# Which weight pieces share a slot in a recurrent attention loop, and who evacuates what

## The chip, the cores and the metric

The kernel runs on one core of a Trainium2 chip. The metric is the device time of one execution in microseconds, the median of three runs: 2337.44 us before the change (2331.31 to 2341.88). The profile is one further execution, with a span of 2344.3 us.

## What is computed

Two branches over the same 2048 tokens of 1024 features are mixed by a gate. The second branch is a plain gated feed-forward. The first is attention over segments of 32 tokens with 8 memory rows that each segment hands to the next, so its 64 segments must run one after the other:

```python
for s in range(n_seg):
    xs = x[:, s * seg_len:(s + 1) * seg_len, :].copy()
    h = jnp.concatenate([mem, xs], axis=1)          # 8 + 32 rows
    q = jnp.einsum('btd,dhe->bhte', h, Wq)          # 32 heads of 128
    k = jnp.einsum('btd,dhe->bhte', h, Wk)
    v = jnp.einsum('btd,dhe->bhte', h, Wv)
    scores = jnp.einsum('bhqe,bhke->bhqk', q, k) * scale
    scores = jnp.where(mask[None, None], scores, -1000000000.0)
    p = _softmax(scores, axis=-1)
    o = jnp.einsum('bhqk,bhke->bhqe', p, v)
    o = jnp.einsum('bhte,hed->btd', o, Wo)
    mem = o[:, :M, :].copy()
    outs.append(o[:, M:, :])
...
g = _sigmoid((x * gate_w).sum(-1, keepdims=True))
return g * a + (1 - g) * b
```

## The kernel before, in words

The program is built in Python by a small recorder (class _Prog): each call of `op` notes an engine, the regions it reads and writes, and from these the waits between engines follow. Work on one engine runs in the order in which it was recorded. Two engines that touch the same PSUM bank are always put one after the other (lines 51 to 55).

**Weights.** Each of Wq, Wk, Wv, Wo is cut into 16 pieces of 512 KB: 8 for each half of the heads (half 0 and half 1). That is 64 pieces, and on-chip memory has 52 slots for them. So 40 pieces stay for the whole loop, and 24 pieces form 12 pairs: piece i of half 0 and piece i of half 1 of the same matrix share a slot. `PAIRS` (line 318) names the paired pieces. As soon as the tensor engine has used the piece in a shared slot, `spent` (after each piece) records the load of its partner on the sync engine's queue, which is served in order. A segment walks one half, then the other; the next segment begins with the half that is in the slots, so that each pair costs one load in a segment: 12 loads, 6.3 MB.

**Order of a segment.** `walk` (line 328) lists the 64 piece steps by hand: k and q of the first half alternating (16 steps), v of the first half (8), k and q of the second half (16), then o of the first half and v of the second half alternating (16), then o of the second half (8). `seq` puts paired pieces first in the first half and last in the second half. Each step is four or eight matmuls on 32-column strips of the array (`proj`).

**What is hung between the steps.** `on(m, r, n, f)` records f ahead of step n of matrix m in half r:

- ahead of the first v step: k is copied from its PSUM bank by ScalarE (ACT), q by VectorE (DVE);
- `turn`, ahead of the fifth v step and of the first o step: k and q are transposed by the tensor engine (`trans8`, line 690), both into bank TT; ACT then copies kT, DVE copies qT (`heads`);
- `scores` and `softmax`: the score matmuls, then a chain of DVE steps with one exponential on ACT, which ends in the transposed probabilities tA (memory and most rows) and tB (the other 8 rows), lines 725 to 742;
- `attend` (line 754) and `attend_tail` (line 766), which need tA, tB and v; their results oT are copied by ACT and DVE in turn;
- "fills": work of a later group of four segments (projections of 8 rows per segment, line 830, and the last o product of earlier rows, line 849) that is independent of the recurrence. `fa` and `fb` hold 8 such steps each, and `some(fa, 2)` puts two of them at that place;
- at the end, the segment's result (bank XO) is copied to a_bf in two halves, the first by ACT and the second by DVE; its 8 memory rows are turned by an identity matmul (line 1027) into hT of the next segment.

The banks are named XO, F2, TT, SS, B0, B1, B2, F1. k goes to B0, q to B1, v of the first half to XO, v of the second half to B0. Behind the loop, the feed-forward takes slices 32 to 40 of the span; the change does not touch it, except that the pieces of Wo which shared a slot are loaded once more near the end (`load_xo`).

Of the kernel before, what the change touches and what calls it, by code (L numbers as in the profile page):

```python
# [30 lines left out]
class _Prog:  # L31
# [47 lines left out]
    def op(self, eng, fn, rd=(), wr=(), lane=None, after=()):  # L79
        o = _Op(eng, fn)  # L80
        if lane is not None:
            ln = self.lanes.get(lane)
            if ln is None:
                ln = self.lanes[lane] = [self.new_sem(f"{self.name}_{lane}"), 0, None]
            if ln[2] is not None:
                o.deps.append(ln[2])
            ln[1] += 16
            o.sem, o.val, o.inc, o.need = ln[0], ln[1], 16, True
            ln[2] = o
        for r in rd:  # L90
            self._touch(o, r, False, lane is not None)
        for r in wr:
            self._touch(o, r, True, lane is not None)
        o.deps.extend(after)
        if eng == "pool" and lane is None:
            if self.pool is not None:
                o.deps.append(self.pool)
            self.pool = o
        for d in o.deps:
            d.need = True  # L100
        o.idx = len(self.ops)
        self.ops.append(o)
        return o
# [92 lines left out]
def bass_gated_mix__memory_aug_recurrent_mem_tr__geglu_ffn__prompt_kernel(  # L196
# [35 lines left out]
    with ExitStack() as es:  # L232
# [23 lines left out]
        PB = [es.enter_context(nc.psum_tensor(f"pb{i}", [128, 512], FP32)) for i in range(8)]  # L256
        PBV = [p[:, :].bitcast(BF16) for p in PB]
# [22 lines left out]
        ident = al("ident", [128, 128])  # L280
# [9 lines left out]
        kT = al("kT", [128, 4, 4, LQ])  # L290
# [3 lines left out]
        tok = al("tok", [128, 512])  # L294
        stage = al("stg", [128, 512])
        pA = al("pA", [128, 8, 32])
        pB = al("pB", [128, 288])
        a_bf = al("a_bf", [128, 256], at=pA.off)
        vAs = [al("vA0", [128, 4, 128], at=oT.off), al("vA1", [128, 4, 128], at=tok.off)]
        qT = al("qT", [128, 4, 4, 32], at=stage.off)  # L300
        tok2 = al("tok2", [128, 512], at=oT.off + 1024)
# [12 lines left out]
        fqk = al("fqk", [128, 4, 2, 128], at=odd0)  # L314
        NSLOT = NLOW + (top - cur[0]) // PIECE


        PAIRS = {"k": (0, 2), "q": (0,), "v": (0, 1, 2, 3), "o": (0, 1, 2, 3, 4)}

        def seq(m, r):  # L320
            pairs = PAIRS[m] if m in "vo" else sorted({*PAIRS["k"], *PAIRS["q"]})
# [2 lines left out]
            return p + f if r == 0 else f + p  # L324
        both = lambda r: [(m, r, i) for i in seq("k", r) for m in "kq"]
        one = lambda m, r: [(m, r, i) for i in seq(m, r)]
        walk = both(0) + one("v", 0) + both(1) + [x for y in zip(one("o", 0), one("v", 1)) for x in y] + one("o", 1)
        spot = {}
        for p, (m, r, i) in enumerate(walk):
            spot.setdefault((m, r), []).append(p)  # L330
# [16 lines left out]
        for s_ in range(NSEG):  # L347
            for p in range(64):
                k = at_step(p, s_)
# [3 lines left out]
        op = P.op  # L353
        BK = lambda b: ("P", b)
        XO, F2, TT, SS, B0, B1, B2, F1 = range(8)
# [43 lines left out]
        for g in range(4):  # L399
            q = slice(32 * g, 32 * g + 32)  # L400
# [136 lines left out]
        def load_v(s, us=(0, 1), eng="sp"):  # L537
# [7 lines left out]
           wr=[gwb.r()], lane="gw")  # L545
# [25 lines left out]
        for T in range(TB):  # L571
            do_x(T)
            load_x(T + NPX)
            if T == 0:
                op("dve", lambda e: e.tensor_copy(hT[:, :, NR:32], memT[:, :].rearrange("p (k c) -> p k c", k=KC)),
                   rd=[memT.r()], wr=[hT.r()])
                op("dve", lambda e: e.tensor_copy(hT[:, :, 0:NR], xTp[0][:, 0, 0, :, 0:NR]),
                   rd=[xTp[0].r(0, KC * SEG)], wr=[hT.r()])
# [3 lines left out]
        for fb in range(NFB):  # L582
            for j in range(NJP):
# [8 lines left out]
                if T == NT:  # L592
                    op("act", lambda e: e.activation(gal[:, :], dl[:, :], ACTF.Exp, scale=-1.0), rd=[dl.r()], wr=[gal.r()])
                    op("dve", lambda e: e.tensor_scalar(out=dl[:, :], in0=gal[:, :], scalar1=1.0, scalar2=None, op0=ALU.add),
                       rd=[gal.r()], wr=[dl.r()])
# [79 lines left out]
        def act_copy(o, i, rd, wr):  # L675
            op("act", lambda e: e.activation(o, i, ACTF.Copy), rd=rd, wr=wr)  # L676
# [4 lines left out]
        cp = {"act": act_copy, "dve": dve_copy}  # L681

        def evac(bank, t, eng="act", lo=0, hi=512):
            cp[eng](t[:, lo:hi] if len(t.h.shape) == 2 else t[:, lo // 128:hi // 128, :].rearrange("p j c -> p (j c)"),
                    PB[bank][:, lo:hi], [BK(bank)], [t.r(lo, hi)])

        def trans4(e, t=tok, head=False, x=0):
            for j in range(4):
                to = PBV[TT][:, x:x + 512].rearrange("p (g j y) -> p j g y", g=4, j=4)[:, j] if head else PBV[TT][:, x + j * 128:x + (j + 1) * 128]
                ins = e.transpose(to, t[:, j * 128:(j + 1) * 128], ident[:, :])  # L690
            return ins

        def trans8(ka, qa, head=False):
            def f(e):
                trans4(e, ka)
                return trans4(e, qa, head, 512)
            op("pe", f, rd=[ka.r(), qa.r(), ident.r()], wr=[BK(TT)])

        def heads(to, eng, x):
            i_ap = PBV[TT][:, x:x + 512].rearrange("p (j g c) -> p (j g) c", g=4, c=32)  # L700
            cp[eng](to[:, :, :, 0:32].rearrange("p j g c -> p (j g) c"), i_ap, [BK(TT)], [to.r()])

        sS = PB[SS][:, 0:320].rearrange("p (a c) -> p a c", a=8)
        nm, sm = st8[:, 0, :], st8[:, 1, :]
# [2 lines left out]
        def scores(u):  # L707

            def f(e):
                for g in range(4):  # L710
                    q = slice(32 * g, 32 * g + 32)
                    e.matmul(PB[SS][q, 0:320].rearrange("p (a c) -> p a c", a=4), lhsT=ident[:, q],
                             rhs=mS[:, :].unsqueeze(1).to_broadcast([128, 4, 80]), start=True, stop=False, skip_group_check=True)
                for j in range(4):
                    for g in range(4):
                        e.matmul(PB[SS][32 * g:32 * g + 32, j * 80:j * 80 + LQ], lhsT=qT[:, j, g, :], rhs=kT[:, j, g, :],
                                 start=False, stop=True, skip_group_check=True)
                for g in range(4):
                    ins = e.matmul(PB[SS][32 * g:32 * g + 32, 0:320].rearrange("p (a c) -> p a c", a=4)[:, :, LQ:80],  # L719
                                   lhsT=qkr[:, u, 0, 32 * g:32 * g + 32], rhs=kT[:, :, g, :],  # L720
                                   start=False, stop=True, skip_group_check=True)
                return ins
            op("pe", f, rd=[qT.r(), kT.r(), ident.r(), mS.r(), qkr.r(256 * u, 256 * u + 128)], wr=[BK(SS)])
            op("pool", lambda e: e.memset(pB[:, :].bitcast(FP32), 0.0), wr=[pB.r()])
            op("dve", lambda e: e.tensor_reduce(nm, sS, AX.X, ALU.max, negate=True), rd=[BK(SS)], wr=[st8.r(0, 8)])  # L725
            op("dve", lambda e: e.tensor_tensor(out=sS, in0=sS, in1=b8(nm, LQ), op=ALU.add), rd=[BK(SS), st8.r(0, 8)], wr=[BK(SS)])  # L726
# [53 lines left out]
        bank_of = {("k", 0): B0, ("q", 0): B1, ("k", 1): B0, ("q", 1): B1, ("v", 0): XO, ("v", 1): B0}  # L780
# [81 lines left out]
                                                      t[32 * g:32 * g + 32, 0:256]),  # L862
                   rd=[t.r(0, 256)] + [("D", "a", x) for x in range(4 * Q, 4 * Q + 4)], wr=[("D", "ar", Q, g)], lane=f"ar{g}")

        def fill_put(ap, r, how, x=0):
            cp[how](ap.rearrange("p i (x c) -> p x i c", x=16), PBV[TT][:, x:x + 512].rearrange("p (x i c) -> p x i c", x=16, i=4),
                    [BK(TT)], [r])

        def store_v(u, G, st, eng="act"):
            op(eng, lambda e: e.dma_start(v_scr[4 * G:4 * G + 4, :, u].rearrange("s i (g j) c -> g (s i) (j c)", g=4), st[:, :]), rd=[st.r()],  # L870
# [31 lines left out]
        for s in range(NSEG):  # L902
            last = s == NSEG - 1
            at = {}
            ua, ub = s % 2, 1 - s % 2
# [9 lines left out]
            def on(m, r, n, *fs):  # L915
                at.setdefault(spot["k" if m == "q" else m, r][n], []).extend(fs)
# [6 lines left out]
            def some(fs, n=99):  # L923
                return lambda: run(fs, n)
# [40 lines left out]

            def turn():
                trans8(tok, stage)
                heads(kT, "act", 0)
                heads(qT, "dve", 512)
            on("v", 0, 4, turn)  # L970
            on("k", 1, 0, lambda: evac(bank_of["v", 0], vAs[0]))
            on("k", 1, 1, lambda: scores(ua))
            on("k", 1, 1, softmax)
            on("k", 1, 5, lambda: rest_k(ub))
            if uw is not None:
                on("k", 1, 5, lambda: load_oR(Q, uw))

            on("o", 0, 0, lambda: evac(bank_of["k", 1], tok))
            on("o", 0, 0, lambda: evac(bank_of["q", 1], stage, "dve"))
            on("o", 0, 0, some(fa, 2))  # L980
            on("o", 0, 0, lambda: attend(ua, 0))
            on("o", 0, 0, lambda: attend_tail(ua, 0))
            on("o", 0, 0, some(fa, 1))
            on("o", 0, 0, turn)
            on("o", 0, 3, lambda: scores(ub))
            on("o", 0, 3, softmax)

            def halves(bank, t):
                evac(bank, t, "act", 0, 256)
                evac(bank, t, "dve", 256, 512)  # L990
            on("o", 1, 0, lambda: halves(bank_of["v", 1], vAs[1]))
            on("o", 1, 0, some(fa))
            on("o", 1, 0, lambda: attend(ub, 1))
            on("o", 1, 0, lambda: attend_tail(ub, 1))
# [20 lines left out]
            for p in range(64):  # L1015
                run(at.get(p, []))
                proj(p, s)
            for t, eng in enumerate(("act", "dve")):
                cs = slice(128 * t, 128 * t + 128)
                cp[eng](a_bf[:, cs], PB[XO][:, cs], [BK(XO)], [a_bf.r(cs.start, cs.stop)])  # L1020
            run(fb, 2)
            if not last:
                for t, bk, eng in ((0, B2, "dve"), (1, SS, "act")):
# [17 lines left out]
            if k1:  # L1041
                pend.append((0, [lambda: evac(F1, tok2), lambda: evac(F2, tok, "dve")]))

                def fills_in(u=k1[1], G=G):
                    trans8(tok2, tok, True)
                    fill_put(fqk[:, :, 1, :], fqk.r(), "act")
                    fill_put(fqk[:, :, 0, :], fqk.r(), "dve", 512)
                    store_qk(u, G, fqk)
                pend.append((3, [fills_in]))
            if uw == 0:  # L1050
# [51 lines left out]
        for fb in range(NFB):  # L1102
            HB, DN = ((0, 1, 2, 3), (4, 5, 6, 7)) if fb % 2 == 0 else ((4, 5, 6, 7), (0, 1, 2, 3))
            for j in range(NJR):
                if fb == 0 and j == sum(CH[:2]):
                    last_tail()
                c, cc = jch[j][0], jch[j][1] * 128
# [90 lines left out]
```

## Time and profile before

| what | value | where |
|---|---|---|
| span of the profiled execution | 2344.3 us | page, head |
| mean granted tensor-engine clock | 0.960 | cores |
| loads of Wo / Wv / Wk / Wq into slots | 331 / 268 / 142 / 79, of 512 KB | page, part 6 |
| median time from issue to landing | 6.9 / 8.0 / 6.8 / 6.7 us | page, part 6 |
| matmul of 512 columns on a strip (L800) | 394 ns mean | page, part 5 |
| ACT copy of 128x512 from PSUM (L676, tok) | 598 ns | page, part 5 |
| DVE copy of 128x512 from PSUM (L679, stg) | 673 ns | page, part 5 |
| ACT and DVE copies of half a v (vA, 128x256) | 384 and 385 ns | groups by form |
| DVE copy of qT, 128x512 bf16 | 425 ns | groups by form |
| DVE idle for qT until ACT had copied kT | 131.4 us, 128 times | waits |
| DVE idle for a_bf until ACT had copied its half | 336.5 us, 64 times | waits |

The page's second part cuts the span into 40 equal slices and gives each engine's busy share in tenths; PEclk is the clock that was granted to the tensor engine, DMA the mean busy share of the 16 DMA engines. The waits view sums the idle time of an engine just ahead of a line by what ended it: total in us, how many times, and the longest. A stage table gives busy us and instruction counts of each engine in stretches of time. A busy tensor engine is not an engine at its peak: a matmul of 512 columns is shown with about 380 ns, while the next four start every 215 ns.

### The profile page before, as it was taken

What the parts mean: (1) busy time and instruction counts of PE and PEld (TensorE: products, weight loads), DVE (VectorE), ACT (ScalarE), POOL (GpSimd) and SP (SyncE); (2) the same over time, 40 slices, a digit from 0 to 9 for tenths busy, and PEclk for the clock granted to TensorE, in tenths of its full rate; (3) what the DMA queues carried; (4) which work ended last, traced back from release to release, by engine and by line L of the source; (5) the groups of instructions that cost most, each with busy time, mean ns of one, the idle gap of its engine ahead of it and who ended that gap; (6) DMA issues with size and microseconds to landing.
All of it is one profiled execution on the core that took longest, in us unless ns stands there. A gap on an engine that the chain in (4) does not pass through costs nothing.

```text
span 2344.3 us, 77525 instructions
## 1 busy us (share of the span) xinstructions
PE 2057.8 (88%) x38218; PEld 944.3 (40%) x32556; DVE 1014.3 (43%) x2248; ACT 601.1 (26%) x1266; POOL 294.1 (13%) x589
## 2 busy tenths in 40 slices
PE   7778888888888888888888888888887999999999
PEld 4334444344444444444444434344333434334343
DVE  6334443444444443444444433444334535345262
ACT  4222222222222222222222222222222312213130
POOL 7110111111111111111101111011101000000000
PEclk9989999999999999999999999999988999999999
DMA  9977787787878878787888877788779900001000
GB/s 369 353 253 264 266 276 260 247 286 260 285 248 267 273 267 268 250 282 275 274 260 277 284 261 255 256 288 284 249 249 309 327 31 28 28 25 40 19 27 19
DMA packets 275695, 529.84 MB, mean 226 GB/s; under 512 B 56080, under 2 KB 109200, under 8 KB 275368
## 3 DMA queue, kind: packets, MB, share of 16 engines
q1 hardware_dynamic: 232640, 484.20, 60.5%
q10 hardware_dynamic: 34136, 20.19, 3.0%
q0 software_dynamic: 8592, 20.49, 2.4%
q8 instruction: 278, 4.55, 0.8%
q14 instruction: 49, 0.40, 0.0%
HBM read 491.21 MB, written 33.55 MB: 224 GB/s over the span
## 4 chain that ended last, share of the span: by engine, by line
PE 58%; DMA 28%; DVE 10%; ACT 2%; issue 1%; POOL 0%; SPq 0%; ACTq 0%; POOLq 0%; DVEq 0%
DMA sl<-in_A_Wo_dram 22%; PE pb L462 15%; PE pb L800 14%; PE pb L783 10%; PE pb L811 5%; PE pb L690 4%; PE pb L1153 4%; PE pb L830 2%; DMA sl<-in_A_Wk_dram 2%; DVE pb L726 1%; DVE st L725 1%; PE pb L849 1%; DVE st L731 1%; DMA qkr<-qk_scr 1%; DVE tB L742 1%
## 5 line engine op out<-in xcount | busy, mean ns | idle before, releaser
L800 PE MATMUL pb<-sl,hT 128*32 128x512 bf16 x8192 | 751.5, 394 | 4.8 <-DMA sl<-in_A_Wk_dram 2.6
L811 PE MATMUL pb<-sl,oT 128*32 128x256 bf16 x8192 | 365.4, 277 | 153.8 <-DMA sl<-in_A_Wo_dram 142.0
L783 PE MATMUL pb<-sl,hT 128*32 128x512 bf16 x4096 | 422.6, 403 | 0.0
L800 PEld LDWEIGHTS pb<-sl,hT 128*32 128x32 bf16 x8192 | 219.7, 100 | 372.4 <-issue 296.1
L811 PEld LDWEIGHTS pb<-sl,oT 128*32 128x32 bf16 x8192 | 199.2, 97 | 260.6 <-DMA sl<-in_A_Wo_dram 161.1
L830 PE MATMUL pb<-sl,hR 128*32 128x512 bf16 x3072 | 228.0, 400 | 11.1 <-ACT stv L676 7.0
L676 ACT ACTIVATE tok<-pb 128x512 bf16<-128x512 f32 x192 | 114.9, 598 | 302.1 <-PE pb L800 276.4
L462 PE MATMUL pb<-xT,wg 128*128 128x512 bf16 x768 | 183.2, 382 | 4.3 <-DMA wg<-in_B_w_gate_dram 4.3
L462 PE MATMUL pb<-xT,wu 128*128 128x512 bf16 x768 | 181.9, 380 | 0.0
L777 POOL COPY oRc<-oT 128x128 bf16<-128x128 bf16 x128 | 98.2, 767 | 636.2 <-DVE oT L679 636.2
L679 DVE CAST stg<-pb 128x512 bf16<-128x512 f32 x128 | 86.1, 673 | 195.1 <-PE pb L783 195.1
L679 DVE CAST a_bf<-pb 128x128 bf16<-128x128 f32 x64 | 18.6, 291 | 336.5 <-ACT a_bf L676 336.5
L1153 PE MATMUL pb<-wd,GT 128*32 128x512 bf16 x1568 | 152.2, 379 | 0.0
L783 PE MATMUL pb<-wd,GT 128*32 128x512 bf16 x1568 | 152.2, 379 | 0.0
L450 ACT ACTIVATE s<-pb 128x512 f32<-128x512 f32 x112 | 67.0, 598 | 291.3 <-PE pb L462 291.3
L451 DVE SCALAR_TENSOR_TENSOR tp<-s,pb 128x512 f32<-128x512 f32 x112 | 76.7, 685 | 123.1 <-ACT s L450 122.7
L676 ACT ACTIVATE oT<-pb 128x256 bf16<-128x256 f32 x256 | 84.3, 381 | 175.6 <-PE pb L766 175.6
L895 POOL COPY kT<-qkr 128x128 bf16<-128x128 bf16 x128 | 37.7, 295 | 676.1 <-PE pb L719 484.1
L462 PEld LDWEIGHTS pb<-xT,wg 128*128 128x128 bf16 x768 | 75.0, 98 | 97.1 <-issue 8.3
L830 PEld LDWEIGHTS pb<-sl,hR 128*32 128x32 bf16 x3072 | 79.4, 98 | 84.8 <-issue 19.9
L729 ACT ACTIVATE E<-pb 128x320 bf16<-128x320 f32 x128 | 56.0, 438 | 219.0 <-DVE pb L726 219.0
L462 PEld LDWEIGHTS pb<-xT,wu 128*128 128x128 bf16 x768 | 75.3, 98 | 91.3 <-issue 1.1
(108 smaller groups left out, 2157.3 us busy)
## 6 DMA issues: line engine op xcount, KB each, us to landing
sl<-in_A_Wo_dram SPq DMA_DIRECT2D x331, 512.0 KB, 6.9
sl<-in_A_Wv_dram SPq DMA_DIRECT2D x268, 512.0 KB, 8.0
sl<-in_A_Wk_dram SPq DMA_DIRECT2D x142, 512.0 KB, 6.8
sl<-in_A_Wq_dram SPq DMA_DIRECT2D x79, 512.0 KB, 6.7
qkr<-qk_scr SPq DMA_DIRECT2D x63, 128.0 KB, 8.4
qk_scr<-fqk ACTq DMA_DIRECT2D x29, 256.0 KB, 6.7
wd<-in_B_w_down_dram SPq DMA_DIRECT2D x7, 1024.0 KB, 14.9
xq_scr<-xTp SPq DMA_DIRECT2D x4, 1024.0 KB, 16.6
```

The costliest lines, as they stand in the source:

```text
L450: op("act", lambda e: e.activation(s1[:, :], hg, ACTF.Square, scale=SQ), rd=[BK(bg)], wr=[s1.r()])
L451: op("dve", lambda e: e.scalar_tensor_tensor(out=t[:, :], in0=s1[:, :], scalar=1.0, in1=hg, op0=ALU.add, op1=ALU.mult), rd=[BK(bg), s1.r() ...
L462: ins = e.matmul(PB[bk][:, 0:FB], lhsT=w[:, kc, cc:cc + 128], rhs=x[:, :, :, kc, :].rearrange("p t i c -> p (t i) c"), start=(kc == 0), st ...
L676: op("act", lambda e: e.activation(o, i, ACTF.Copy), rd=rd, wr=wr)
L679: op("dve", lambda e: e.tensor_copy(o, i), rd=rd, wr=wr)
L690: ins = e.transpose(to, t[:, j * 128:(j + 1) * 128], ident[:, :])
L777: op("pool", lambda e: e.tensor_copy(oRc[:, u, :, :].rearrange("p c (g j) -> p g j c", g=4), diag), rd=[oT.r()], wr=[oRc.r(128 * u, 128 * ...
L783: return e.add_instruction(mybir.InstMatmult(name=nc.get_next_instruction_name(), start_tensor_calc=start, stop_tensor_calc=stop, tile_siz ...
L800: ins = again(e, g, *at, one, end) if k[0] == "q" else e.matmul(*at, start=one, stop=end)
L811: ins = e.matmul(PB[XO][32 * g:32 * g + 32, 0:256], lhsT=oT[:, gp_, 2 * jj + hh, 0:32], rhs=w[:, c:c + 256], start=(r == 0 and one and hh ...
L830: ins = e.matmul(PB[b][32 * g:32 * g + 32, :], lhsT=h[:, k[2], :], rhs=w[:, g * 512:(g + 1) * 512], start=(n == 0), stop=(n == 7))
L1153: ins = again(e, q, *a, j == 0, j == NJ - 1) if hf else e.matmul(*a, start=(j == 0), stop=(j == NJ - 1))
```

## The change

Which pieces share a slot changes: three of k, none of q, six of v and three of o, again 12 pairs. The mixed run of o and v is no longer strictly alternating: most of the second half's v steps stand behind the o steps, so that loads of v have longer until they are wanted. q is transposed into its own bank (B1, and B2 for the fills), so that kT and qT can be copied at the same time. Three evacuations go from two engines, or from DVE, to ACT alone: the second half's q, the second half's v, and a_bf. The scores of the first half are recorded two steps earlier, and three fill steps instead of two stand ahead of the first attention, none behind it.

```diff
-        PAIRS = {"k": (0, 2), "q": (0,), "v": (0, 1, 2, 3), "o": (0, 1, 2, 3, 4)}
+        PAIRS = {"k": (0, 2, 4), "q": (), "v": (0, 1, 2, 3, 4, 6), "o": (0, 1, 2)}
...
-        walk = both(0) + one("v", 0) + both(1) + [x for y in zip(one("o", 0), one("v", 1)) for x in y] + one("o", 1)
+        O0, V1 = one("o", 0), one("v", 1)
+        walk = both(0) + one("v", 0) + both(1) + O0[0:3] + V1[0:1] + O0[3:6] + V1[1:2] + O0[6:8] + V1[2:8] + one("o", 1)
...
-        def trans8(ka, qa, head=False):
+        def trans8(ka, qa, head=False, tq=B1):
             def f(e):
                 trans4(e, ka)
-                return trans4(e, qa, head, 512)
-            op("pe", f, rd=[ka.r(), qa.r(), ident.r()], wr=[BK(TT)])
+                return trans4(e, qa, head, tq)
+            op("pe", f, rd=[ka.r(), qa.r(), ident.r()], wr=[BK(TT), BK(tq)])
...
             def turn():
                 trans8(tok, stage)
-                heads(kT, "act", 0)
-                heads(qT, "dve", 512)
+                heads(kT, "act", TT)
+                heads(qT, "dve", B1)
...
-            on("k", 1, 1, lambda: scores(ua))
-            on("k", 1, 1, softmax)
+            on("k", 1, 0, lambda: scores(ua))
+            on("k", 1, 0, softmax)
...
-            on("o", 0, 0, lambda: evac(bank_of["q", 1], stage, "dve"))
-            on("o", 0, 0, some(fa, 2))
+            on("o", 0, 0, lambda: evac(bank_of["q", 1], stage))
+            on("o", 0, 0, some(fa, 3))
             on("o", 0, 0, lambda: attend(ua, 0))
             on("o", 0, 0, lambda: attend_tail(ua, 0))
-            on("o", 0, 0, some(fa, 1))
             on("o", 0, 0, turn)
...
-            def halves(bank, t):
-                evac(bank, t, "act", 0, 256)
-                evac(bank, t, "dve", 256, 512)
-            on("o", 1, 0, lambda: halves(bank_of["v", 1], vAs[1]))
+            on("o", 1, 0, lambda: evac(bank_of["v", 1], vAs[1]))
...
-            for t, eng in enumerate(("act", "dve")):
-                cs = slice(128 * t, 128 * t + 128)
-                cp[eng](a_bf[:, cs], PB[XO][:, cs], [BK(XO)], [a_bf.r(cs.start, cs.stop)])
+            act_copy(a_bf[:, :], PB[XO][:, 0:256], [BK(XO)], [a_bf.r()])
...
-                    trans8(tok2, tok, True)
+                    trans8(tok2, tok, True, B2)
                     fill_put(fqk[:, :, 1, :], fqk.r(), "act")
-                    fill_put(fqk[:, :, 0, :], fqk.r(), "dve", 512)
+                    fill_put(fqk[:, :, 0, :], fqk.r(), "dve", B2)
```

More of the change, by code (lines that the diff above doesn't have):

```diff
@@ L685, in evac, with trans4, heads @@
                     PB[bank][:, lo:hi], [BK(bank)], [t.r(lo, hi)])
-        def trans4(e, t=tok, head=False, x=0):
+        def trans4(e, t=tok, head=False, b=TT):
             for j in range(4):
-                to = PBV[TT][:, x:x + 512].rearrange("p (g j y) -> p j g y", g=4, j=4)[:, j] if head else PBV[TT][:, x + j * 128:x + (j + 1) * 128]
+                to = PBV[b][:, 0:512].rearrange("p (g j y) -> p j g y", g=4, j=4)[:, j] if head else PBV[b][:, j * 128:(j + 1) * 128]
                 ins = e.transpose(to, t[:, j * 128:(j + 1) * 128], ident[:, :])
             return ins
-        def trans8(ka, qa, head=False):
+        def trans8(ka, qa, head=False, tq=B1):
             def f(e):
                 trans4(e, ka)
-                return trans4(e, qa, head, 512)
-            op("pe", f, rd=[ka.r(), qa.r(), ident.r()], wr=[BK(TT)])
-        def heads(to, eng, x):
-            i_ap = PBV[TT][:, x:x + 512].rearrange("p (j g c) -> p (j g) c", g=4, c=32)
-            cp[eng](to[:, :, :, 0:32].rearrange("p j g c -> p (j g) c"), i_ap, [BK(TT)], [to.r()])
+                return trans4(e, qa, head, tq)
+            op("pe", f, rd=[ka.r(), qa.r(), ident.r()], wr=[BK(TT), BK(tq)])
+        def heads(to, eng, b):
+            i_ap = PBV[b][:, 0:512].rearrange("p (j g c) -> p (j g) c", g=4, c=32)
+            cp[eng](to[:, :, :, 0:32].rearrange("p j g c -> p (j g) c"), i_ap, [BK(b)], [to.r()])
         sS = PB[SS][:, 0:320].rearrange("p (a c) -> p a c", a=8)
@@ L863, in store_tail, with fill_put @@
                    rd=[t.r(0, 256)] + [("D", "a", x) for x in range(4 * Q, 4 * Q + 4)], wr=[("D", "ar", Q, g)], lane=f"ar{g}")
-        def fill_put(ap, r, how, x=0):
-            cp[how](ap.rearrange("p i (x c) -> p x i c", x=16), PBV[TT][:, x:x + 512].rearrange("p (x i c) -> p x i c", x=16, i=4),
-                    [BK(TT)], [r])
+        def fill_put(ap, r, how, b=TT):
+            cp[how](ap.rearrange("p i (x c) -> p x i c", x=16), PBV[b][:, 0:512].rearrange("p (x i c) -> p x i c", x=16, i=4),
+                    [BK(b)], [r])
         def store_v(u, G, st, eng="act"):
```

## The prediction

> **What bounds the kernel now.** I read the page first: slices, then the chain that ended last, because a PE at 88% busy beside a DMA at 70 to 80% does not say which of them sets the end.
>
> ```profile
> PE 2057.8 (88%) x38218; PEld 944.3 (40%) x32556; DVE 1014.3 (43%) x2248; ACT 601.1 (26%) x1266; POOL 294.1 (13%) x589
> PEclk9989999999999999999999999999988999999999
> DMA  9977787787878878787888877788779900001000
> PE 58%; DMA 28%; DVE 10%; ACT 2%; issue 1%; POOL 0%; SPq 0%; ACTq 0%; POOLq 0%; DVEq 0%
> ```
>
> The reader is to see two regimes (a loop up to slice 31, a DMA-free feed-forward after it, untouched by the change), and that in the loop 28% of the whole chain is DMA. The a_bf line of the tile view counts the loop: 64 segments, ends from 143.0 to 1801.8 us, so 1658.8 / 63 = 26.33 us each.
>
> ```profile
> L676 ACT ACTIVATE a_bf<-pb x64: 277/278/278, 143.0 to 1801.8; 128x128 bf16<-128x128 f32 x64
> ```
>
> Next, what PE waits for in the loop (waits of PE, 250 to 1700 us, some 55 segments):
>
> ```profile
> PE pb L811 <- DMA sl<-in_A_Wo_dram: 124.1, 131, 2.6
> PE pb L754 <- DVE vA L679: 49.8, 54, 1.9
> PE pb L766 <- DVE tB L742: 10.3, 50, 0.2
> ```
>
> Per segment: 124.1/55 = 2.26 us for Wo pieces, 0.91 us for the half of v1 that VectorE evacuates late, 0.19 us for tB. Last, one segment by stage: k/q of the first half, v, k/q of the second half, attention, the mixed o/v run, attention, o of the second half, its end.
>
> ```profile
> core 0: us, PE busy (x) PEld busy (x) DVE busy (x) ACT busy (x) POOL busy (x), PEclk, DMA share, GB/s
> 1122.00:1126.60 4.60, 4.60 (x76) 0.97 (x36) 0.00 (x0) 0.40 (x2) 0.00 (x0) 0.76 0.67 148
> 1126.60:1129.40 2.80, 2.80 (x54) 1.26 (x46) 1.11 (x2) 1.39 (x3) 0.00 (x0) 1.00 0.94 361
> 1129.40:1132.70 3.30, 3.30 (x84) 1.05 (x53) 2.13 (x6) 0.82 (x2) 0.86 (x2) 1.00 1.01 367
> 1132.70:1134.90 2.20, 2.00 (x48) 0.95 (x41) 2.17 (x6) 1.25 (x3) 0.00 (x0) 1.00 0.97 376
> 1134.90:1139.40 4.50, 4.50 (x137) 3.23 (x140) 2.53 (x7) 1.42 (x3) 0.99 (x2) 1.00 0.73 256
> 1139.40:1142.20 2.80, 1.85 (x63) 1.14 (x59) 2.10 (x7) 0.91 (x3) 0.09 (x1) 1.00 0.96 347
> 1142.20:1146.00 3.80, 2.26 (x77) 1.69 (x72) 0.00 (x0) 0.24 (x1) 0.86 (x2) 1.00 0.93 302
> 1146.00:1147.80 1.80, 1.68 (x60) 1.04 (x44) 0.69 (x3) 0.48 (x2) 0.00 (x0) 1.00 0.17 47
> ```
>
> PE is idle in three stages only; the DMA has slack only at the start and end of a segment and a dent (0.73) in the mixed run. The timeline shows the waits:
>
> ```profile
> 1140.87 0.29 PE L754 MATMUL pb<-tA,vA 32*128 32x64 bf16 x16 [0.95 <-DVE vA L679]
> 1144.24 0.40 PE L811 MATMUL pb<-sl,oT 128*32 128x256 bf16 x8 [0.46 <-DMA sl<-in_A_Wo_dram]
> 1145.73 0.40 PE L811 MATMUL pb<-sl,oT 128*32 128x256 bf16 x8 [1.08 <-DMA sl<-in_A_Wo_dram]
> ```
>
> I then took issue and landing of every weight load from the trace, as means over segments 4 to 59, counted from the segment's first k matmul. First k load lands at 5.58; then, step by step, 1.98 and 1.52 (q, k), 2.08, 1.52, 1.44, 1.34 (v), 2.21, 1.83, 1.77, 1.56, 1.54 (o). The last o lands at 24.39, and the next segment begins 1.90 later. So the end of a segment hangs on the fifth o piece. The chain from first to last landing is 18.8 us, and the 16 DMA engines are busy for 17.05 of it. That is the number that keeps me modest: the wait on Wo is mostly the DMA at its rate, and only in part a matter of order.
>
> **What the Trainium skill says.** "DMA: Bandwidth & Descriptors", Queues, rings and completion order: on each DMA engine a queue's descriptors are taken in ring order. The trace agrees: loads land in order of issue, 1.3 to 2.2 us apart. Its Specifications give about 358 GB/s from HBM per core; the full stages above move 347 to 376, so the measured rate is taken. "TensorE: Matmul & The Clock Gate", Part 1: an idle window of about 3.4 us drops PE to half clock for the next. The trace: half clock comes in pieces of 3.41 us, and after 32 of the 34 such windows with PE under 50% busy, but 3 of 18 with 50 to 60% and none of the warm ones above. "PSUM — Partial Sum Buffer", Specifications: ScalarE and VectorE read at full rate together unless they share a bank; the code serializes them on one bank, and the trace has qT waiting 131.4 us for kT.
>
> **The change part by part.**
>
> *Weight pairs.* 12 loads of 512 KB per segment before (2 k, 1 q, 4 v, 5 o) and after (3, 0, 6, 3): no byte less. What moves is when a load is asked for. Two loads formerly freed in the mixed run are now freed in v (4 and 5 us into a segment, not 14 to 16), so the DMA no longer has the dent before the first o (2.21 against 1.5), and after the three o loads the chain ends.
>
> *PE's own path*, at full clock: a step of four matmuls takes 0.215 us (start to start in the timeline: 1147.34, 1147.56, 1147.78). k and q 16 × 0.215 = 3.44; v 4 steps 0.86, transposes 0.6, 4 steps 0.86; scores 0.35; k and q again 3.44 (to 9.5); 3 fill steps 0.65, attention 0.5. The turn waits for q1: k1 evacuation 0.60 and then q1 0.60 on ACT, so at +1.3, to 10.85; transposes 0.55 (11.4); 16 o/v steps 3.44 and scores 0.31; 5 fills 1.08 (16.2); attention 0.5; 4 fills 0.86; 8 o steps 1.72: 19.3, and 1.55 to the next segment: 20.9 with everything at hand.
>
> *The new waits.* Loads after: k at 5.4, 7.1, 8.6; v at 10.4 in warm segments, then 1.45 to 1.5 apart, so the sixth at about 17.9; three o at 1.5 apart, 22.4. PE wants the last four v at 14.2 to 14.9. It therefore waits there, up to 3 us, first time for v. Behind that matmul in PE's queue stand 5 fills, the attention, 4 fills, all of o; for its result wait ACT's v1 evacuation and the attention. From the sixth v: its own step 0.2, 5 fills 1.08, attention 0.5, 4 fills and the last oT copy 0.95, o 1.72, the rest 1.35, together 5.8 us to the next segment, 23.7. From the last o: 22.4 + 1.6 = 24.0. The two nearly tie; I take 24.1. The third fill now moved ahead of the attention is in half the segments the first v pair (needed about 10.0, landing 10.4 to 11.7): up to 1.5 us of wait in front of the attention, but hidden, as the DMA sets the end.
>
> *Clock.* Three v steps in 3 us leave the window near 40% busy, so a half-clock window (3.41 us, a loss of up to 1.7) can follow, now over fills and o rather than over the next k. With 0.3 us of slack it costs about 1.3. Before, 34 of 62 segments had one; I take 45%, as the fill's wait spreads idle time.
>
> *v1 on ACT alone:* 0.60 instead of 0.38 and then 0.38 behind the softmax. It removes the 0.91 wait, but scores start two steps earlier and lead tB by 4.3 us (scores at 1129.39, tB at 1133.70), to 16.5, just inside the 16.2 + 0.3. *q1 on ACT* saves 0.33 before the turn. *q in its own bank:* qT no longer follows kT, 0.42 earlier; *first scores two steps earlier* uses it. *a on one engine:* 0.38 against 0.28 + 0.29, about 0.1. All except the last lie ahead of the v wait and are hidden by the DMA: I count them at nothing. Same for extra ACT time: 26% busy.
>
> Sum: 0.55 × 24.1 + 0.45 × 25.4 = 24.7 us a segment. 26.33 − 24.7 = 1.63; × 63 = 103; 2337 − 103 = 2235.
>
> The unseen quantity is the step between loads in an unbroken queue of nine. From below 1.34 (the last v step), from above 1.77 (a middle o step); I take 1.5. Over the 8 steps behind the first v that is −1.3 to +2.2 us a segment, −80 to +136 us; the upper end is the less likely, because the o steps of before hold late issues of their own: o pieces were freed one by one between v steps.
>
> **Rivals.**
> - *Packed and warm*: steps near 1.4, no dips: last o at 10.4 + 8 × 1.4 = 21.6, + 1.6, + 0.3 for stores that only some segments have (the mean segment is 26.28, the lightest kind 25.93): T 23.5, 2337 − 2.83 × 63 = 2159. For: segments without a dip already end in 24.4 (35, 39, 55). Against: 17.05 of busy DMA in the chain.
> - *DMA stays the bound*: steps near 1.7, last o at 24.0, + 1.7: T 25.7, 2337 − 0.63 × 63 = 2297. For: the chain is 91% busy already; against: the steps in it that are longest are those where a queue ran dry.
> - *No gain*: chain unchanged, T 26.2 to 26.4, about 2337.
> - *Late v with cold PE*, slower: the sixth v at the old mean, 15.46 + 2 × 1.7 = 18.9, + 5.8 + 1.7 of half clock, + 0.4 if it reaches into the next k: 26.8, 2337 + 0.5 × 63 = 2367. For: six v in a row are a longer burst than any before; against: half clock then mostly ends before the next k.
>
> **How the numbers follow.** Mine 0.50, packed 0.19, DMA-bound 0.18, no gain 0.05, slower 0.08. Faster 0.87, same 0.05, slower 0.08. The time is mine, 2235. From 2165 to 2320 leaves out the fastest edge of packed, no gain and slower, under 2 in 10.
>
> **What would show it.** Right: the waits on Wo at L811 fall below 40 us, a wait of L800 on Wv appears (over 50 us), the wait on vA vanishes, DMA share in the loop rises from 0.79 to about 0.84, half clock moves off k. Wrong: waits on Wo stay above 100 us (the chain was the rate), or PE in the loop exceeds 95% (the DMA had more to give), or half clock in nearly every segment.

## The result and the profile after

The changed kernel takes 2186.08 us (median of four runs, 2183.66 to 2193.13) against 2336.76 us: a ratio of 0.936, 95% interval 0.933 to 0.939. The forecast was 2235 us, in a range from 2165 to 2320. So the direction and the mechanism held, and the gain, 151 us, came out half as large again as the 102 that were forecast.

The page after, second and fourth part: PE's clock, the DMA's busy share in 40 slices, and the shares of the chain that ended last.

```profile
PEclk9999999999999999999999999999998999999999
DMA  9988888888888888888878888888889200000000
PE 63%; DMA 31%; issue 2%; ACT 1%; DVE 1%; SPq 1%; POOL 0%; ACTq 0%; POOLq 0%; DVEq 0%
DMA sl<-in_A_Wv_dram 26%; PE pb L463 16%; PE pb L801 13%; PE pb L784 10%; PE pb L812 6%; PE pb L831 5%; PE pb L1148 4%; PE pb L691 3%; PE pb L850 3%; DMA sl<-in_A_Wo_dram 2%; PE pb L1126 1%; SPq L379 1%; DMA xr_scr<-xr 1%; ACT a_bf L677 1%;
```

The reader is to see that the DMA's share of the chain did not go away. It changed its name: Wv has 26% where Wo had 22%. The DMA is busier in nearly every slice of the loop (0.85 instead of 0.80 between 250 and 1400 us), since the same 12 loads now fit into less time. That stretch before and after (us, busy us of PE, PE's weight loads, DVE, ACT and POOL with counts, then the clock, the DMA share and GB/s):

```profile
250.00:1400.00 1150.00, 993.11 (x22612) 480.20 (x19796) 490.90 (x1240) 306.28 (x691) 153.28 (x340) 0.96 0.80 268
250.00:1400.00 1150.00, 1041.40 (x24920) 523.54 (x21840) 484.33 (x1221) 372.85 (x808) 167.99 (x374) 0.99 0.85 297
```

The tile view of a_bf gives the loop:

```profile
L677 ACT ACTIVATE a_bf<-pb x64: 384/384/385, 143.8 to 1643.5; 128x256 bf16<-128x256 f32 x64
```

1643.5 − 143.8 = 1499.7 us for 63 segments is 23.80 us each, where there were 26.33. 2.53 × 63 = 159 us, which is all of the difference of the two profiled spans (2344.3 − 2184.8 = 159.5). Outside the loop next to nothing moved.

PE's waits between 250 and 1600 us (total us, times, longest), first before, with some 51 segments in that stretch:

```profile
PE pb L811 <- DMA sl<-in_A_Wo_dram: 114.5, 120, 2.6
PE pb L754 <- DVE vA L679: 45.3, 50, 1.0
PE pb L766 <- DVE tB L742: 9.7, 47, 0.2
PE pb L811 <- issue: 8.7, 9, 1.8
```

then after, with some 57:

```profile
PE pb L801 <- DMA sl<-in_A_Wv_dram: 74.9, 97, 1.9
PE pb L812 <- issue: 19.6, 25, 1.4
PE pb L831 <- DMA sl<-in_A_Wv_dram: 4.9, 6, 1.2
PE pb L755 <- ACT vA L677: 2.1, 3, 0.7
PE pb L812 <- DMA sl<-in_A_Wo_dram: 1.5, 4, 0.6
```

The wait for Wo is all but gone, so are the one for vA (2.1 us are left, now for ACT) and the one for tB, and a new wait for Wv of 1.3 us a segment stands in their place. "Issue" marks time in which PE waited for nothing that the profile shows. Segment 47 by stage (columns as above), and its waits in the timeline:

```profile
1240.60:1244.10 3.50, 3.50 (x76) 0.97 (x40) 0.42 (x1) 0.02 (x1) 2.54 (x5) 1.00 0.62 136
1244.10:1246.40 2.30, 2.30 (x44) 1.08 (x36) 1.12 (x2) 1.18 (x2) 0.38 (x2) 1.00 0.98 371
1246.40:1250.30 3.90, 3.90 (x100) 1.30 (x64) 2.66 (x7) 1.10 (x3) 0.29 (x1) 1.00 0.99 327
1250.30:1251.90 1.60, 1.58 (x44) 0.82 (x36) 0.94 (x3) 1.52 (x4) 0.00 (x0) 1.00 1.02 415
1251.90:1255.50 3.60, 3.36 (x110) 2.38 (x108) 2.18 (x6) 1.17 (x3) 0.97 (x2) 1.00 1.02 408
1255.50:1258.20 2.70, 1.10 (x17) 0.33 (x16) 1.52 (x5) 0.00 (x0) 0.00 (x0) 1.00 1.04 398
1258.20:1261.00 2.80, 2.80 (x72) 1.24 (x68) 0.76 (x2) 1.26 (x3) 0.27 (x1) 1.00 0.85 292
1261.00:1262.50 1.50, 1.50 (x67) 1.36 (x58) 0.00 (x0) 0.00 (x0) 0.49 (x1) 1.00 0.32 86
```

```profile
1255.26 0.82 PE L801 MATMUL pb<-sl,hT 128*32 128x512 bf16 x9 [0.24 <-issue]
1256.81 0.40 PE L801 MATMUL pb<-sl,hT 128*32 128x512 bf16 x4 [0.73 <-DMA sl<-in_A_Wv_dram]
1258.08 0.40 PE L801 MATMUL pb<-sl,hT 128*32 128x512 bf16 x4 [0.88 <-DMA sl<-in_A_Wv_dram]
1260.72 1.95 PE L812 MATMUL pb<-sl,oT 128*32 128x256 bf16 x64
```

The dent of the DMA in the mixed run (0.73 before) is filled (1.02), the idle stretch of PE is the one before the last two v steps, and all eight o steps of the second half run in one piece. PE's busy share of the stage with the waits is 1.10 of 2.70 us, and the clock still stays at 1.00.

From the issue and landing of each load in the trace, means over segments 4 to 59 in us, counted from the segment's first k matmul: first k lands at 5.10 (5.58 before), first v at 10.43 (11.17), last v at 17.64 (15.47, when it was the fourth), last o at 21.85 (24.39). The next segment begins 1.98 later, and 6.19 after the last v.

### The profile page after: what moved, and what is told of

Its sections match the earlier page's. It is cut to its first block, busy times and chain, and to the rows that moved or that the text cites. A ratio compares the mean times of both kernels' runs of the same rounds, so it can differ in the third digit from the quotient of the medians.

```text
span 2184.8 us, 77490 instructions
## 1 busy us (share of the span) xinstructions
PE 1992.8 (91%) x38220; PEld 938.7 (43%) x32556; DVE 938.7 (43%) x2056; ACT 650.0 (30%) x1330; POOL 293.0 (13%) x589
## 4 chain that ended last, share of the span: by engine, by line
PE 63%; DMA 31%; issue 2%; ACT 1%; DVE 1%; SPq 1%; POOL 0%; ACTq 0%; POOLq 0%; DVEq 0%
DMA sl<-in_A_Wv_dram 26%; PE pb L463 16%; PE pb L801 13%; PE pb L784 10%; PE pb L812 6%; PE pb L831 5%; PE pb L1148 4%; PE pb L691 3%; PE pb L850 3%; DMA sl<-in_A_Wo_dram 2%; PE pb L1126 1%; SPq L379 1%; DMA xr_scr<-xr 1%; ACT a_bf L677 1%; PE pb L755 1%
## 5 line engine op out<-in xcount | busy, mean ns | idle before, releaser
L801 PE MATMUL pb<-sl,hT 128*32 128x512 bf16 x8192 | 708.6, 381 | 98.3 <-DMA sl<-in_A_Wv_dram 83.7
L784 PE MATMUL pb<-sl,hT 128*32 128x512 bf16 x4096 | 399.5, 379 | 0.0
L812 PE MATMUL pb<-sl,oT 128*32 128x256 bf16 x8192 | 287.0, 277 | 28.2 <-issue 21.3
L812 PEld LDWEIGHTS pb<-sl,oT 128*32 128x32 bf16 x8192 | 210.3, 98 | 72.1 <-issue 31.4
L831 PE MATMUL pb<-sl,hR 128*32 128x512 bf16 x3072 | 218.1, 394 | 19.6 <-DMA sl<-in_A_Wv_dram 10.7
L680 DVE CAST oT<-pb 128x256 bf16<-128x256 f32 x256 | 96.8, 420 | 203.9 <-PE pb L767 203.9
L677 ACT ACTIVATE vA<-pb 128x512 bf16<-128x512 f32 x128 | 76.4, 597 | 226.1 <-PE pb L801 226.1
L831 PEld LDWEIGHTS pb<-sl,hR 128*32 128x32 bf16 x3072 | 79.3, 98 | 103.9 <-issue 28.5
L726 DVE TENSOR_REDUCE st<-pb 128x8 f32<-128x320 f32 x128 | 63.0, 492 | 125.8 <-PE pb L720 125.7
L680 DVE CAST stg<-pb 128x512 bf16<-128x512 f32 x64 | 44.3, 692 | 155.2 <-PE pb L784 155.2
L455 DVE SCALAR_TENSOR_TENSOR tp<-tp,pb 128x512 f32<-128x512 f32 x112 | 77.0, 688 | 78.9 <-ACT tp L454 77.4
```

The lines of the kernel that those rows point to most:

```text
L455: op("dve", lambda e: e.scalar_tensor_tensor(out=t[:, :], in0=t[:, :], scalar=1.0, in1=hu, op0=ALU.add, op1=ALU.mult), rd=[BK(bu), t.r()], ...
L680: op("dve", lambda e: e.tensor_copy(o, i), rd=rd, wr=wr)
L784: return e.add_instruction(mybir.InstMatmult(name=nc.get_next_instruction_name(), start_tensor_calc=start, stop_tensor_calc=stop, tile_siz ...
L801: ins = again(e, g, *at, one, end) if k[0] == "q" else e.matmul(*at, start=one, stop=end)
L812: ins = e.matmul(PB[XO][32 * g:32 * g + 32, 0:256], lhsT=oT[:, gp_, 2 * jj + hh, 0:32], rhs=w[:, c:c + 256], start=(r == 0 and one and hh ...
L831: ins = e.matmul(PB[b][32 * g:32 * g + 32, :], lhsT=h[:, k[2], :], rhs=w[:, g * 512:(g + 1) * 512], start=(n == 0), stop=(n == 7))
```

## The experiments

Theory A is the forecast's: the gain is the order of the loads; what else was changed lies ahead of the wait for v and is hidden.

**One part at a time.** The first two parts of the diff above, `PAIRS` (the pairs) and `walk` (the new run of o and v), on the kernel before:

> The kernel before with the new pairs and the new order of the o/v run alone; evacuations, banks, fills and scores as before. Theory A (the gain is the loads' order: everything else lies ahead of the wait for the last v and is hidden): 2190 to 2210, at most 20 us above the full change. Rival B (the shorter path through evacuations and banks carries a good part): 2235 to 2265, since v1's half that VectorE copies late (0.9 us a segment before) now lies behind the last v, where nothing hides it.

The full change with those two set back:

> The full change with the old pairs and the old alternating run: only evacuations, banks, fills and scores are changed. Theory A: 2320 to 2337, because the last o load still sets the end of a segment. Rival B: 2270 to 2290.

`PAIRS` alone, on the kernel before:

> The kernel before with the new pairs alone, o and v still alternating. Theory A: within 20 us of the pairs with the new run (2190 to 2230), as the last v step stands at the same place, sixteenth of the run, in both orders, and only the first pairs are wanted earlier. Rival (the order of the run is what lets v arrive): over 2260.

`walk` alone, on the kernel before:

> The kernel before with the new order of the run and the old pairs. The five o loads are asked for up to 1 us earlier. Theory A: 2295 to 2330. Rival (order is what counts): below 2260.

| kernel | us | ratio to before, 95% |
|---|---|---|
| pairs and run | 2196.79 | 0.942 (0.938 to 0.946) |
| all but pairs and run | 2312.58 | 0.992 (0.989 to 0.996) |
| pairs alone | 2195.69 | 0.941 (0.935 to 0.947) |
| run alone | 2335.72 | 1.001 (0.998 to 1.004) |
| all | 2186.08 | 0.936 (0.933 to 0.939) |

The first four were measured beside a kernel before of 2334.76 us, the last row is the main result, beside 2336.76. One line of the diff, the pairs, gives 139 us; all of it gives 151. Both kernels with the new pairs came where theory A had them, far below rival B. With the pairs alone PE waits for Wv, and only 0.9 us in all for Wo (250 to 1600 us, as above):

```profile
PE pb L800 <- DMA sl<-in_A_Wv_dram: 78.9, 125, 1.9
PE pb L754 <- DVE vA L679: 2.8, 3, 0.9
```

The line changes k and q as well as v and o; these two halves of it were not run apart. The pairs also take most of the half clock away (between segments 3 and 60 it lasts 139 us before and 24 us with the pairs alone), so a part of the gain can be the clock's; the filler experiment below bears on it. That an o load as such takes longer than a v load is not the reason: after the change the o loads land 1.40 us apart, the v loads 1.44.

The new run gives nothing, with the new pairs or with the old, where theory A had allowed it 5 to 40 us: in the alternating run the last v step is also the sixteenth. The evacuations, banks and fills give 22 us by themselves (2312.58, just below the 2320 to 2337 of theory A and above the 2270 to 2290 of rival B), and with the new pairs about 10, where the intervals overlap. By themselves, with the old pairs, the segment's waits were

```profile
PE pb L811 <- DMA sl<-in_A_Wo_dram: 102.7, 118, 2.5
PE pb L811 <- issue: 30.7, 27, 3.7
PE pb L766 <- DVE tB L742: 5.8, 29, 0.2
```

so the wait for vA went, the one for Wo lost little, and the one for nothing that the profile shows grew (8.7 before). The o loads are asked for 0.2 to 0.3 us sooner, and the last lands at 24.03 instead of 24.39.

**What the row of loads is worth.** Two single loads left out of the kernel after, then all. In each the condition is added to the line that asks for the partner of a spent piece, so the slot keeps its first piece and part of the products use the wrong weights:

```diff
-            if done[n] < len(uses[n]) and uses[n][done[n]] != k:
+            if done[n] < len(uses[n]) and uses[n][done[n]] != k and not (k[0] == "k" and k[2] == 4):
```

> The kernel after without the loads of the k pair 4 in the loop (its slot keeps its first piece, so half of those products use the wrong weights). Eleven loads instead of twelve, and all v and o land one step of 1.4 us earlier. Theory A (the row of loads sets the segment): -1.4 x 63 = -88, 2090 to 2110. Rival (PE's own path sets it): 2165 to 2186.

Measured 2173.02 us, ratio 0.932 (0.929 to 0.936): 13 us less than after, with intervals that overlap, and not 88. Theory A in its plain form falls. The time lies in the rival's range, but PE's own path is not what sets it either, as the run without any load shows below (1996 us). The landings say why so little was gained: the last k lands 2.1 us earlier (6.39 instead of 8.53), but the first v only at 9.90 instead of 10.43. It lands 5.67 us after it was asked for although less stood ahead of it in the queue.

With `k[0] == "o" and k[2] == 2`:

> The kernel after without the loads of the last o pair (2) in the loop (its slot keeps its first piece). Nothing ahead of it moves. Theory A, in the form that the sixth v with the work behind it and the last o nearly tie: -5 to -25, 2160 to 2180. Rival (the last o alone sets the end): -88, about 2098.

2176.79 us, ratio 0.932 (0.927 to 0.937), 9 us less, again with overlapping intervals. The last o now lands at 20.43 instead of 21.85, and the next segment begins 3.34 behind it instead of 1.98; it begins 6.04 behind the last v, where it had been 6.19. So with the last o out of the way the last v, with the work behind it, still holds the end almost where it was. This is the tie that the forecast worked out: neither of the two loads alone is worth much.

With `True`:

> The kernel after without any load of a paired piece in the loop. What is left is PE's own path: worked out as 20.9 us a segment, 2186 - 2.9 x 63 = 2003. Rival (waits on other engines, or on nothing that the profile shows, come out when loads are gone): over 2060.

1996.15 us. The a_bf line and a stretch of 1150 us (busy us as above, clock, DMA share, GB/s):

```profile
L677 ACT ACTIVATE a_bf<-pb x64: 384/384/385, 133.3 to 1458.3; 128x256 bf16<-128x256 f32 x64
250.00:1400.00 1150.00, 1139.51 (x28152) 589.79 (x24652) 546.69 (x1378) 422.43 (x915) 191.07 (x424) 1.00 0.13 36
```

1325.0 / 63 = 21.03 us a segment, where the step-by-step path of PE had given 20.9, and PE is busy for 99% of the stretch. So the evacuations and the softmax leave PE next to nothing to wait for (its longest wait is 3.2 us in all between 250 and 1600 us), and 23.80 − 21.03 = 2.8 us a segment are still owed to loads.

**What the clock was worth.** On the kernel before, matmuls of no use ahead of each of the last three o steps:

```diff
+                if r == 1 and i in (2, 3, 4):
+                    wf = slots[home["k", 0, 7]]
+
+                    def busy(e):
+                        for _ in range(3):
+                            for g in range(4):
+                                ins = e.matmul(PB[TT][32 * g:32 * g + 32, :], lhsT=ident[:, 0:32], rhs=wf[:, 0:512], start=True, stop=True)
+                        return ins
+                    op("pe", busy, rd=[ident.r(), wf.r()], wr=[BK(TT)])
```

> The kernel before with 12 matmuls of no use (0.65 us) ahead of each of the last three o steps, where PE waits for Wo, so that its clock stays up. Theory A with a part for the clock: half-clock windows fall from 41 to under 10, and with them up to 1.7 us each in segments that had one; 2280 to 2310. Rival (loads set the end, the clock costs nothing): 2325 to 2355, as the filler only takes the place of waits or adds to them.

2314.02 us, ratio 0.991 (0.988 to 0.993), between the two expectations. The clock stayed up (1.00, where the same stretch before has 0.96):

```profile
250.00:1400.00 1150.00, 1048.94 (x24418) 537.71 (x21561) 496.74 (x1250) 308.85 (x697) 153.88 (x342) 1.00 0.81 272
```

Between segments 3 and 60 the half-clock time fell from 139 to 10 us, but the time by 20 us only, filler included. The last o landed at 23.99 instead of 24.39. So the half clock cost the kernel before at least these 20 us and was not the main thing: the loads still set the end.

**Other splits of the twelve.** One v pair of the kernel after made into an o pair or into a k pair, and the kernel after beside them:

```diff
-        PAIRS = {"k": (0, 2, 4), "q": (), "v": (0, 1, 2, 3, 4, 6), "o": (0, 1, 2)}
+        PAIRS = {"k": (0, 2, 4), "q": (), "v": (0, 1, 2, 3, 4), "o": (0, 1, 2, 3)}
```

> The kernel after with one v pair turned into an o pair (3 k, 5 v, 4 o), twelve loads as before. Theory C (the first v lands some 6 us after it is asked for, and from there each load takes 1.44; whichever of the last v with 6 us of work behind it and the last o with 1.5 comes later sets the end): last v at 16.2, so 22.3; last o unchanged at 21.9, so 23.4; 23.83 to 23.4 is 27 us, 2150 to 2170. Rival (the number of loads alone sets the end): 2180 to 2190, no change.

```diff
-        PAIRS = {"k": (0, 2, 4), "q": (), "v": (0, 1, 2, 3, 4, 6), "o": (0, 1, 2)}
+        PAIRS = {"k": (0, 2, 4, 6), "q": (), "v": (0, 1, 2, 3, 4), "o": (0, 1, 2)}
```

> The kernel after with one v pair turned into a k pair (4 k, 5 v, 3 o). A fourth k load fills the stretch in which the queue now waits for the first v. Theory C: first v at 11.4, last v at 17.1, so 23.1; last o at 21.4, so 22.9; 23.83 to 23.1 is 45 us, 2130 to 2160, if the fourth k, landing near 10.0 and wanted near 9.1, delays only what has slack. Rival (a late k holds up the second half's scores, and so everything): 2190 to 2230.

> The kernel after, unchanged, so that the two others can be compared with it on the same chip: 2180 to 2195.

| k, v, o pairs | us | ratio to before, 95% | last k, last v, last o land |
|---|---|---|---|
| 3, 5, 4 | 2201.91 | 0.944 (0.941 to 0.947) | 8.60, 16.33, 22.28 |
| 4, 5, 3 | 2167.23 | 0.928 (0.926 to 0.931) | 10.23, 17.31, 21.59 |
| 3, 6, 3 (after) | 2185.58 | 0.936 (0.933 to 0.940) | 8.43, 17.69, 21.83 |

The number of loads alone does not set the end: equal numbers differ by 35 us. But theory C missed the first case: it expected a gain of 27 us, and the kernel is 16 us slower than after. It had the last v right (16.2 forecast) and the last o wrong by 0.4: four o take 5.95 us from the last v to the last o, 1.49 each, where the v loads take 1.44. The next segment then begins 1.77 us behind the last o, where 1.5 had been taken. The waits move back to Wo, and the waits for nothing that the profile shows are at their largest:

```profile
PE pb L812 <- DMA sl<-in_A_Wo_dram: 35.9, 51, 1.1
PE pb L812 <- issue: 34.6, 34, 2.4
PE pb L801 <- DMA sl<-in_A_Wv_dram: 22.8, 40, 1.5
```

In the second case the fourth k comes late, as expected, and PE waits for it, but its waits for v shrink: k and v together are 78.7 us, where they were 77.7 after.

```profile
PE pb L801 <- DMA sl<-in_A_Wv_dram: 44.8, 60, 2.3
PE pb L801 <- DMA sl<-in_A_Wk_dram: 33.9, 51, 2.4
```

It is faster than both other kernels, by 0.8% of after, with intervals that don't overlap. The size was 18 us, where 25 to 55 had been expected. The last v and the last o land 0.38 and 0.24 us earlier; the half clock between segments 3 and 60 is also less, 10 us against 31 in the kernel after beside it, and what each is worth here was not taken apart.

**Asking for v earlier.** The first two v steps moved ahead of the last k and q steps:

```diff
-        walk = both(0) + one("v", 0) + both(1) + O0[0:3] + V1[0:1] + O0[3:6] + V1[1:2] + O0[6:8] + V1[2:8] + one("o", 1)
+        K0, V0 = both(0), one("v", 0)
+        walk = K0[0:10] + V0[0:2] + K0[10:16] + V0[2:8] + both(1) + O0[0:3] + V1[0:1] + O0[3:6] + V1[1:2] + O0[6:8] + V1[2:8] + one("o", 1)
-            on("v", 0, 0, lambda: evac(bank_of["k", 0], tok))
-            on("v", 0, 0, lambda: evac(bank_of["q", 0], stage, "dve"))
+            on("v", 0, 2, lambda: evac(bank_of["k", 0], tok))
+            on("v", 0, 2, lambda: evac(bank_of["q", 0], stage, "dve"))
-            on("v", 0, 4, turn)
+            on("v", 0, 6, turn)
```

> The kernel after with the first two v steps of the first half moved ahead of the last six k and q steps (evacuations and turn keep their distance to the end of v). The first v load is asked for near 2.4 us instead of 4.2. Theory C (the time of asking starts the row of v): the first v lands right behind the third k, near 9.9 instead of 10.4, the last v 0.5 earlier; 2150 to 2172. Rival (queue and stores set the first v, as other transfers fill that stretch): it lands at 10.4 as before, 2180 to 2200.

2183.91 us, ratio 0.935 (0.933 to 0.938): no difference to after. The first v was asked for at 3.02 instead of 4.23 and landed at 10.49 instead of 10.43; the last v landed at 17.61. The rival's number is right here, and its reason is not: between the last k and the first v lie 1.78 us, and for 1.72 of them the DMA engines work on packets of the weights' own queue, not on other transfers. Together with the skipped k load this says that neither the time of asking nor the place in the queue alone paces the first v: taking a load out ahead of it gains 0.5 us, asking 1.2 us earlier gains nothing.

## Why the prediction came out as it did

**What bounds the kernel: right.** Wo's last load set the end, and asking for two of the loads earlier took that wait away (114.5 to 1.5 us). The pairs alone show it.

**The new wait: right in place, and close in size.** First v forecast at 10.4, measured 10.43; last v 17.9 against 17.64; from there 5.8 against 6.19 on average, with 5.6 as the least. "The two nearly tie" was right: with the landings as measured, the forecast's own sums give 17.64 + 5.8 = 23.44 for the v and 21.85 + 1.6 = 23.45 for the o.

**"I take 1.5" and the segment of 24.1 us: mis-sized by 0.55 us.** From the first v to the last o the loads came 1.43 us apart, so that the last o landed at 21.85 instead of 22.4. (The first k was earlier too, 5.10 instead of 5.4, but that did not pass on to the first v.) The 48 of segments 4 to 59 that had no half clock took 23.55 us on average.

**"Clock": the share was three times too high, the cost about right.** The forecast put half clock into 45% of the segments. Measured: 27 us of half clock between segments 3 and 60, that is 8 windows of 3.41 us in 8 segments, 14% of them. (Before, 40 of segments 1 to 62 had one, not the 34 that the forecast counted.) The rule that the forecast read from the trace held, and the windows did not come: of the windows of 3.41 us between segments 3 and 60, 34 had PE under 50% busy before, and 33 of them were followed by half clock; after, there were 9, of which 7 were followed, and another 13 with 50 to 55%, of which one was. PE's idle time is now cut into shorter waits (in segment 47 0.24, 0.73 and 0.88 us). The 8 segments took 25.54 us, forecast 25.4. They are also those where the loads came late (last v at 18.16 instead of 17.56), but from the last v on they took 7.38 us against 5.99 in the others, 1.4 us more, where 1.3 had been forecast.

Together: 0.86 × 23.55 + 0.14 × 25.54 = 23.8 us instead of 24.7. Some 0.5 us of the difference come from the segment at full clock, 0.4 from the share of half clock.

**The rival "packed and warm" came closer than the forecast.** It had steps near 1.4 us, the last o at 21.6, no half clock and 2159 us. The result, 1.43, 21.85, half clock in 14% and 2186 us, is 27 us from it and 49 us from 2235. The forecast gave it 0.19 and itself 0.50, because the DMA engines were busy for 17.05 us of the chain of loads. That was the wrong ground: the chain from first to last landing shrank from 18.8 to 16.75 us, less than this busy time, and the engines are busy for 15.97 us of it. The weight loads in it have the same bytes, and all that was moved in it fell only from 5933 to 5747 KB. So "the wait on Wo is mostly the DMA at its rate" was too dark: busy engines were not engines at their best.

**Edits counted at nothing: nearly right.** With the new pairs they are worth about 10 us in 2186, within the intervals; by themselves 22, where the last o also lands 0.36 us sooner. The forecast gave the end of the wait for vA to ACT copying all of v; the pairs alone end it too (2.8 us left of 45.3), although DVE still copies half of v there. PE's own path, 20.9 us, was confirmed by the run without loads, 21.03.

**The third fill in front of the attention: right, smaller than feared.** L831 waited 4.9 us for Wv in all, against up to 1.5 us in half the segments: PE reaches the third fill 10.0 or 10.7 us into most segments, hardly earlier than the first v lands.

**The new run** had no number of its own in the forecast, which told it as part of what gives v more time. It is worth nothing.

Of the signs named in advance, all came: Wo under 40 us, Wv over 50 (74.9), vA gone, DMA share at 0.85, half clock off k (none of the 8 windows reaches the next segment's k).

## What to carry to other kernels

When loads in a queue set the end of an iteration, ask when each of them is asked for, not only how many there are: twelve loads of the same bytes took 26.3 or 23.8 us a segment by which pieces share a slot, and one more shift, from v to k, gave a further 18 us. Price each removed wait together with the one that comes up behind it; here two paths ended within half a microsecond of each other, so that leaving out one load gained 13 or 9 us. The kernel with all these loads left out gives the floor, and it agreed with a path added up from the timeline to 1%.

## What the runs showed that was not expected

The first v load takes 5.7 us from asking to landing with one k load less ahead of it and 6.2 with it, and doesn't land earlier when asked for 1.2 us earlier. What paces it was not settled. Between the last k and the first v landing the DMA engines are busy for 1.88 of 1.90 us, and without that k load for 3.21 of 3.51 us, so their packets take longer there. Nearly all of it (1.86 and 3.16 us) are packets of the weights' own queue, so other transfers of this core do not fill that stretch; its packets of 4 KB take 197 and 234 ns on average, against 161 ns between the first and the last v of the kernel after. Why they do stays open.

PE's waits at L812 for nothing that the profile shows are between 8 and 35 us in the kernels with loads (8.7 before, 19.6 after, 34.6 with four o pairs), and in the run without loads they are not among its longest waits, of which the one for nothing shown is 2.2 us, at another line. That they come with loads is likely from this; why they differ so much between kernels with equal numbers of loads was not settled. The kernel after, profiled twice, has 19.6 and 12.8 us, so a part of it differs from run to run.
